# DeltaNet and SwiGLU on one core: splitting float64 weights with a ScalarE multiply and an integer add

## The chip, the cores and the metric

The kernel runs on one core of a Trainium2 chip. The metric is the device time of one execution in microseconds (us). Engines are called as in the profile: PE (TensorE, matrix products; PEld is its weight load), DVE (VectorE), ACT (ScalarE), POOL (GpSimd) and SP (SyncE, which here only issues DMA transfers). A "q" behind a name (SPq, ACTq) is that engine's own instruction queue.

## The reference

Two blocks run one behind the other. The first is a recurrent attention (DeltaNet) over 768 steps for 4 batches and 8 heads of 48; its output is regrouped into 3072 tokens of 384 and goes through a normalised SwiGLU feed-forward of width 1536.

```python
k_n = k / (np.linalg.norm(k, axis=-1, keepdims=True) + 1e-06)
for t in range(S):
    y[:, :, t] = np.einsum('bhd,bhde->bhe', q[:, :, t], state)
    v_old = np.einsum('bhde,bhd->bhe', state, kt)
    state = state + bt[:, :, :, None] * np.einsum('bhd,bhe->bhde', kt, vt - v_old)
...
xn = x / np.sqrt(np.mean(x * x, axis=-1, keepdims=True) + 1e-06) * rms_g
g = xn @ w_gate
out = (g * (1.0 / (1.0 + np.exp(-g))) * (xn @ w_val)) @ w_out
```

The three weight matrices (`w_gate` and `w_val` 384 x 1536, `w_out` 1536 x 384) arrive as float64. The kernel computes in float32, so it has to turn each weight into a float32, and there is no float64 arithmetic on the engines: the two 32-bit words of each number are worked on apart.

## The kernel before, in words

**Chunks.** The 768 steps are cut into 12 chunks of 64 (`NCH`). For each chunk, `prep(c)` solves the small triangular systems inside the chunk, `qpart(c)` makes the masked scores of q, and `recur(c)` applies the chunk to the running state and makes the chunk's rows of x, which are 256 tokens. Each chunk's tokens then go through the feed-forward: `ffn_plain` for chunks 0 and 1 (L1094 up, L1076 down) and `ffn` with `down` for the others (L1187 and L1244), which use sums and differences of weight blocks made by `factors` and `out_factors` and so fewer products.

**The preparation of a chunk** is a chain over many engines. The scores of k (L546) go out to DRAM (buffer dkk) and come back in another layout as `at` (L659). VectorE scales `at` (L665) and solves the system in a scan of 15 steps, two instructions each (L712 and L718), some 16 us in all. ScalarE copies the result apart (L735, only the first two chunks use it in this form), it goes to DRAM (buffer dx) and comes back in small transfers as `mt` (for chunk 1 `mt` lies in the tile `wsum`, so the profile says wsum) and `x2bd`. PE turns a block (L770), VectorE and ScalarE copy it to `m1bd` (L783, L781), two merges follow on PE (L794 and L818) with copies behind them (L804; L832 and L834), and `mt` is whole. Then `recur` multiplies it with the residual (L905), copies to `u` (L942, L944), multiplies by the scores (L919), and brings the rows to unit mean square (L981 or L987 and L993, root on POOL L1006, scaling L1014 or L1021); PE turns them (L1027), ScalarE scales them by the weights of the norm (L1031), and the feed-forward can begin.

**The weights** are loaded in 18 pieces of 768 KB (`weights`, loads 0 to 17) through three raw buffers (`raw`, number n mod 3) and two pairs of conversion buffers (`cva` and `cvb`, n mod 2). In a float64, the upper word has the sign, 11 bits of exponent and 20 of mantissa; the lower word has the other 32 bits of mantissa. Before the change a load is converted in four or five steps:

- ScalarE (L467) reads the upper word as if it were a float32 and scales it by a power of two, another one for negative numbers (a Prelu), which puts the exponent, and the sign with it, where they should be after a shift.
- VectorE (L455) shifts that word left by three. Now it is the float32 of the weight with its mantissa cut at 20 bits: `top`.
- VectorE (L458) masks sign and exponent of `top` into `cc`.
- VectorE (L463) multiplies the lower word (taken as a number) by 2**-52 and by `cc`: the part of the weight that was cut off.
- The two parts are added: for the first three loads by two PE products with the identity into one PSUM bank (L480, L481) and a ScalarE copy out of it (L485), for the other 15 by one VectorE add (L488).

A raw buffer is free for the next load once L463 has read it.

**The order of the work** is not that of the code. Each operation is put on a list with an engine, an estimated duration, a priority, the data it reads and writes and the PSUM banks it takes (`Plan.add`). `Plan.run` plans all engines forward and backward 60 times, with small random shakes of the priorities from a fixed seed, and writes out the order with the earliest planned end; each engine, and SP's queue of transfers, then runs its instructions strictly in that order. So an operation that is added or removed, or whose estimate changes, can move any other. Up to a planned 70 us, the holes that the plan leaves on PE are filled with products of the identity with itself (`filler`, L1344), which keep it busy and compute nothing.

Of the kernel before, what the change touches and what calls it, by code (L numbers as in the profile page):

```python
# [12 lines left out]
U32 = mybir.dt.uint32  # L13
I64 = mybir.dt.int64
ALU = mybir.AluOpType
# [234 lines left out]
def kernel(  # L250
# [17 lines left out]
    nc = tc.nc  # L268
# [14 lines left out]
    def sbt(name, shape, n=None, dt=FP32):  # L283
        if n is None:
            return sb.tile(shape, dt, name=name)
        return [sb.tile(shape, dt, name=f"{name}{i}") for i in range(n)]

    ident = sbt("ident", [128, 128])
# [15 lines left out]
    NPE, NRAW, NCV = 3, 3, 2  # L304
# [39 lines left out]
    tmp = sbt("tmp", [128, 6, 512])  # L344
# [4 lines left out]
    raw = [more[:, 1536 * i : 1536 * i + 1536].bitcast(I64) for i in range(NRAW)]  # L349
    cvb = [tflat[:, 512:1280], more[:, 4608:5376]]  # L350
    cva = [xf[:, 6:12].rearrange("p a n -> p (a n)"), more[:, 5376:6144]]
# [9 lines left out]
    P = Plan()  # L361
    V = lambda n: 0.13 + 0.0011 * n
    VF = lambda n: 0.13 + 0.0006 * n
    A = lambda n: 0.2 + 0.0008 * n
    G = lambda n: 0.15 + 0.0022 * n

    def dma(dst, src, prio, r=(), w=(), work=0.3, dur=0.5, eng="SP", after=0.0):
        queue = nc.scalar if eng == "ACT" else nc.sync
        op = P.add(eng, dur, lambda: queue.dma_start(out=dst, in_=src), prio, r, w, lat=0.7)  # L369
        op.dma, op.work, op.ready = True, work, after  # L370
# [50 lines left out]
    def spot(f):  # L421

        return f // 6 * 6 + (0, 1, 4, 5, 2, 3)[f % 6]


    def weights():
        todo = []
        for half_ in range(2):
            c0 = half_ * WCOL

            for i_ in range(3):
                for side, (key, w) in enumerate((("wg", moe_w_gate), ("wv", moe_w_val))):
                    c1 = c0 + 256 * i_
                    src = w.rearrange("(t p) c -> p t c", p=128)[:, :, c1 : c1 + 256]
                    todo.append((w_in[:, side, half_, i_:9:3], src, [(key, half_, i_)]))
                if i_:
                    for f in ((6 * half_,) if i_ == 1 else (6 * half_ + 2, 6 * half_ + 4)):
                        src = moe_w_out[f * 128 : f * 128 + 256, :].rearrange("(a p) c -> p a c", a=2)
                        z = spot(f)
                        todo.append((wo_sb[:, z : z + 2], src, [("wo", f), ("wo", f + 1)]))  # L440
        for n, (dst, src, keys) in enumerate(todo):
            pr = (30 if n < 9 else CV2) + 0.2 * n
            i, a = n % NRAW, n % NCV
            parts = dst.shape[1]
            rdst = raw[i].rearrange("p (a c) -> p a c", a=parts)
            dma(rdst, src, (0.1 if n == 0 else 3 + 2 * n), w=[("raw", i)], dur=0.7, work=3.06, after=(7.5, 5.0, 19.2, 27.2, 24.5, 33.3, 47.0)[n] if n < 7 else 48.8)

            low, high = (raw[i].bitcast(U32)[:, w_ : w_ + 2 * WCOL - 1 : 2] for w_ in range(2))
            top, cc = cva[a], cvb[a]
            u = top.bitcast(U32)  # L450
            tiled = lambda t: t.rearrange("p (a n) -> p a n", a=parts)
            cak, cvk = [("cva", a)], [("o", 1)] if a else [("tmp", 1), ("tmp", 2)]

            def s2(u=u):
                nc.vector.tensor_scalar(out=u, in0=u, scalar1=3, scalar2=None, op0=ALU.logical_shift_left)  # L455

            def s4(u=u, cc=cc):
                nc.vector.tensor_scalar(  # L458
                    out=cc.bitcast(U32), in0=u, scalar1=0xFF800000, scalar2=None, op0=ALU.bitwise_and
                )  # L460

            def s5(low=low, cc=cc, by=2.0**-52):
                nc.vector.scalar_tensor_tensor(out=cc, in0=low, scalar=by, in1=cc, op0=ALU.mult, op1=ALU.mult)  # L463

            P.add("ACT", 0.84, lambda high=high, top=top: nc.scalar.activation(out=top, in_=high.bitcast(FP32), func=ACTF.Prelu, scale=2.0**-112, alpha=2.0**32), pr, r=[("raw", i)], w=cak)  # L467
            P.add("DVE", 0.57, s2, pr, w=cak)
            P.add("DVE", 0.57, s4, pr, r=cak, w=cvk)
            P.add("DVE", 0.96, s5, pr, r=[("raw", i)], w=cvk)  # L470
            done = []
            if n < NPE:
                for x_ in range(2):
                    ps = Group()
                    cut = slice(2 * x_, 2 + x_)
                    flat = slice(512 * x_, 512 + 256 * x_)
                    m = 512 - 256 * x_

                    def s6(ps=ps, top=top[:, flat], cc=cc[:, flat], m=m):
                        nc.tensor.matmul(ps.t[:, 0:m], ident, top, start=True, stop=False)  # L480
                        nc.tensor.matmul(ps.t[:, 0:m], ident, cc, start=False, stop=True)  # L481

                    P.add("PE", 0.0035 * m, s6, pr, r=cvk + cak + ["ident"], w=[("cvp", n, x_)], ps=ps, size=8)
                    done.append(("cv", n, x_))
                    P.add("ACT", A(m), lambda dst=dst[:, cut], ps=ps, m=m: nc.scalar.copy(dst, ps.t[:, 0:m].rearrange("p (a n) -> p a n", n=256)), pr, r=[("cvp", n, x_)], w=[done[-1]], last=ps)  # L485
            else:
                done.append(("cv", n))
                P.add("DVE", 0.97, lambda dst=dst, top=tiled(top), cc=tiled(cc): nc.vector.tensor_tensor(out=dst, in0=top, in1=cc, op=ALU.add), pr, r=cvk + cak, w=[done[-1]])  # L488
            for key in keys:
                ready.setdefault(key, []).extend(done)  # L490

# [581 lines left out]
    def down_mm(po, f, f0, f1):  # L1073
        def mm():
            for p in range(2):
                nc.tensor.matmul(  # L1076
                    po[p].t[:, 0:DM], hf[:, spot(f), 128 * p : 128 * p + 128], wo_sb[:, spot(f)], start=(f == f0), stop=(f == f1 - 1),
                    skip_group_check=True,
                )

        return mm

    def ffn_plain(c, f0, f1, start):
        x_, xk = (xp1, [("x1", 0), ("x1", 1)]) if c else (xf, [("xp", 0), ("xp", 1)])
        po = [Group(), Group()]

        def up(f):
            ps = Group()
            h_, i_, n = f // 6, f % 6 // 2, 128 * (f % 2)
            for side, key in enumerate(("wg", "wv")):  # L1090

                def mm(side=side, ps=ps):
                    for t in range(KT):
                        nc.tensor.matmul(  # L1094
                            ps.t[:, TOK * side : TOK * side + TOK], w_in[:, side, h_, 3 * t + i_, n : n + 128],
                            x_[:, 2 * t : 2 * t + 2].rearrange("p a n -> p (a n)"), start=(t == 0), stop=(t == KT - 1)
                        )

                P.add("PE", 1.31, mm, start + 3.9 * (f - f0), r=xk + [("wuse", h_)] + ready[(key, h_, i_)], w=[ps, (("sil", f % 2), ("hf", f, 0))[side]], ps=ps, size=12)
            a = f % 2  # L1100
            P.add("ACT", A(256), lambda ps=ps: nc.scalar.activation(out=sil[a], in_=ps.t[:, 0:TOK], func=ACTF.Silu), -1, r=[ps], w=[("sil", a)], last=ps)
            P.add("DVE", V(256), lambda ps=ps: nc.vector.tensor_tensor(out=hf[:, spot(f)], in0=sil[a], in1=ps.t[:, TOK : 2 * TOK], op=ALU.mult), -1, r=[("sil", a), ps, ("tmp", 0)], w=[("hf", f, 0), ("hf", f, 1)], last=ps)

        def down(f):
            if f == f0:
                P.add("PE", 0.0, lambda: None, start, r=xk + [("cvp", n, x_) for n in range(NPE) for x_ in range(2)], w=["po"], ps=po[1])
            P.add("PE", 1.31, down_mm(po, f, f0, f1), start + 3.9 * (f - f0) + 9, r=[("hf", f, 0), ("hf", f, 1), "wouse"] + ready[("wo", f)], w=["po"], ps=po[0], size=8)

        LAG = 2
        for f in range(f0, f1 + LAG):  # L1110
            if f < f1:
                up(f)
            if f >= f0 + LAG:
                down(f - LAG)
        finish(c, po, f0, f1)
# [179 lines left out]
    load(0, "kqv")  # L1295
    load_small()
    weights()
    load(1, "k")
    P.slack, P.lead = 0.0, 1000.0
# [80 lines left out]
```

## Time and profile before

| | |
|---|---|
| median of 3 runs | 716.01 us (714.25 to 716.3) |
| span of the profiled execution, first to last instruction | 713.4 us |
| PE busy | 694.6 us (97%) |
| DVE busy | 553.9 us (78%) |
| ACT busy | 303.5 us (43%) |
| of PE: fillers (L1344) | 43.1 us |
| VectorE conversion: L455, L458, L463, L488, one each, 128 x 768 | 0.56, 0.56, 0.96, 0.95 us |
| ScalarE conversion: L467, 128 x 768 | 0.92 us |

The span is from the profiled execution alone; its device time is not listed apart, so it is compared with the median of the runs. In a row of the profile, the text names the line, the engine, the operation and the tiles (what is written, an arrow, what is read), then come the shape, the count, the busy time and the mean of one in ns, and at the end the idle time of the engine before these instructions with what ended it. In a row of busy times by stretches, the two times are followed by the length, the busy time of PE, PEld, DVE, ACT and POOL with the number of instructions, the granted PE clock as a share of full speed, the busy share of the DMA engines, and what they moved in GB/s.

### The profile page before, as it was taken

What the parts mean: (1) busy time and instruction counts of PE and PEld (TensorE: products, weight loads), DVE (VectorE), ACT (ScalarE), POOL (GpSimd) and SP (SyncE); (2) the same over time, 40 slices, a digit from 0 to 9 for tenths busy, and PEclk for the clock granted to TensorE, in tenths of its full rate; (3) what the DMA queues carried; (4) which work ended last, traced back from release to release, by engine and by line L of the source; (5) the groups of instructions that cost most, each with busy time, mean ns of one, the idle gap of its engine ahead of it and who ended that gap; (6) DMA issues with size and microseconds to landing.
All of it is one profiled execution on the core that took longest, in us unless ns stands there. A gap on an engine that the chain in (4) does not pass through costs nothing.

```text
span 713.4 us, 23227 instructions
## 1 busy us (share of the span) xinstructions
PE 694.6 (97%) x9950; PEld 630.5 (88%) x9950; DVE 553.9 (78%) x1148; ACT 303.5 (43%) x712; POOL 138.2 (19%) x140
## 2 busy tenths in 40 slices
PE   8999698999999999999999999999999999999997
PEld 5657576787879999999999999999999999999997
DVE  4899788999949949949949959959937969947373
ACT  5335353233415634534525535435345444345231
POOL 4202103102131231231232232232105040100000
PEclk9999889999999999999999999999999999999999
DMA  7886898262540170262451361450461170030000
GB/s 142 229 140 134 174 270 185 32 110 38 94 82 13 26 126 17 49 104 38 65 102 32 61 119 25 77 89 11 62 121 22 16 121 7 21 58 2 23 1 23
DMA packets 232791, 54.67 MB, mean 77 GB/s; under 512 B 221936, under 2 KB 225008, under 8 KB 232688
## 3 DMA queue, kind: packets, MB, share of 16 engines
q1 hardware_dynamic: 227840, 52.27, 39.2%
q10 hardware_dynamic: 4848, 0.92, 0.9%
q8 instruction: 78, 1.28, 0.8%
q14 instruction: 25, 0.20, 0.1%
HBM read 40.83 MB, written 12.32 MB: 75 GB/s over the span
## 4 chain that ended last, share of the span: by engine, by line
PE 84%; DVE 6%; DMA 3%; issue 3%; SPq 2%; POOL 1%; ACT 0%; POOLq 0%; DVEq 0%; ACTq 0%
PE bank L1187 35%; PE bank L1244 19%; PE bank L1094 8%; PE bank L1076 4%; PE bank L546 3%; PE bank L1344 3%; PE bank L859 3%; PE bank L905 2%; PE bank L818 2%; SPq L369 2%; PE bank L919 2%; DVE tmp L1197 1%; PE bank L523 1%; DMA dx<-wsum 1%; PE bank L794 1%
## 5 line engine op out<-in xcount | busy, mean ns | idle before, releaser
L1187 PE MATMUL bank<-xf,w_in 128*128 128x128 f32 x1440 | 180.8, 277 | 0.0
L1197 DVE TENSOR_TENSOR tmp<-tmp,bank 128x512 f32<-128x512 f32 x180 | 121.4, 683 | 69.4 <-PE bank L1187 62.8
L1187 PEld LDWEIGHTS bank<-xf,w_in 128*128 128x128 f32 x1440 | 170.0, 192 | 2.4 <-issue 1.2
L1187 PE MATMUL bank<-xf,more 128*128 128x128 f32 x960 | 125.0, 277 | 0.3 <-DVE tmp L1197 0.3
L1187 PEld LDWEIGHTS bank<-xf,more 128*128 128x128 f32 x960 | 115.4, 192 | 2.3 <-DVE tmp L1197 0.5
L1199 ACT COPY tmp<-bank 128x512 f32<-128x512 f32 x120 | 68.9, 586 | 91.3 <-PE bank L1187 65.6
L718 DVE TENSOR_REDUCE acc<-acc 128x30 f32<-128x90 f32 (+4 forms) x180 | 85.1, 473 | 6.2
L1203 ACT ACTIVATE tmp<-tmp 128x256 f32<-128x256 f32 x120 | 49.8, 418 | 88.0 <-DVE tmp L1197 87.5
L568 POOL TENSOR_TENSOR knrm<-ksum,half 128x16 f32<-128x16 f32 x12 | 36.1, 3011 | 195.9 <-DVE ksum L567 195.9
L712 DVE TENSOR_TENSOR acc<-acc,at 128x60 f32<-128x60 f32 (+4 forms) x180 | 63.2, 351 | 6.5 <-DMA out_dram<-tmp 3.8
L1244 PE MATMUL bank<-wo_sb,hf 128*128 128x192 f32 x360 | 63.9, 327 | 0.0
L1204 DVE TENSOR_TENSOR hf<-tmp 128x256 f32<-128x256 f32 x120 | 52.7, 453 | 7.9 <-ACT tmp L1203 7.3
L1244 PEld LDWEIGHTS bank<-wo_sb,hf 128*128 128x128 f32 x360 | 58.2, 190 | 0.3
L1344 PE MATMUL bank<-ident 128*128 128x128 f32 (+2 forms) x150 | 43.1, 433 | 1.4 <-POOL ident masks.py:199 1.4
L1344 PEld LDWEIGHTS bank<-ident 128*128 128x128 f32 x150 | 25.4, 195 | 17.8 <-issue 15.2
L1094 PE MATMUL bank<-xf,w_in 128*128 128x256 f32 x144 | 36.1, 400 | 3.2 <-issue 2.8
L1094 PEld LDWEIGHTS bank<-xf,w_in 128*128 128x128 f32 x144 | 28.1, 200 | 10.0 <-issue 3.9
L739 POOL COPY acc<-acc 128x128 f32<-128x128 f32 x40 | 19.8, 526 | 85.6 <-DVE acc L718 85.2
L665 POOL TENSOR_TENSOR at<-at,beta_b 128x1024 f32<-128x1024 f32 x8 | 18.8, 2355 | 88.0 <-DMA at<-dkk 63.0
L1076 PE MATMUL bank<-wo_sb,hf 128*128 128x384 f32 x96 | 35.6, 508 | 0.0
L1094 PE MATMUL bank<-xp,w_in 128*128 128x256 f32 x144 | 33.3, 382 | 0.0
L1094 PEld LDWEIGHTS bank<-xp,w_in 128*128 128x128 f32 x144 | 26.8, 190 | 4.5
(167 smaller groups left out, 1006.3 us busy)
## 6 DMA issues: line engine op xcount, KB each, us to landing
at<-dkk SPq DMA_DIRECT2D x23, 256.0 KB, 4.4
more<-in_moe_w_val_dram SPq DMA_DIRECT2D x6, 768.0 KB, 6.5
more<-in_moe_w_gate_dram SPq DMA_DIRECT2D x6, 768.0 KB, 7.2
more<-in_moe_w_out_dram SPq DMA_DIRECT2D x6, 768.0 KB, 7.6
vt<-in_v_dram SPq DMA_DIRECT2D x24, 192.0 KB, 4.5
out_dram<-tmp SPq DMA_DIRECT2D x48, 96.0 KB, 2.2
k<-in_k_dram SPq DMA_DIRECT2D x23, 192.0 KB, 4.0
mt<-dx SPq DMA_DIRECT2D x84, 32.0 KB, 2.1
```

The lines of the kernel that those rows point to most:

```text
L568: P.add("POOL", 2.95, lambda: nc.gpsimd.tensor_tensor(out=knrm[i2], in0=ksum[i2], in1=half, op=ALU.pow), pn, r=[("ksum", i2), "half"], w=[ ...
L712: nc.vector.tensor_tensor(out=acc[:, 1:3, 0:n, j + 2 : W].rearrange("p a i t -> p i a t"), in0=acc[:, old, 0:n, j : j + 2, None].to_broadc ...
L718: nc.vector.tensor_reduce(out=acc[:, new, 0:n, j + 2 : W], in_=acc[:, lo : lo + 3, 0:n, j + 2 : W].rearrange("p a i t -> p i t a"), axis=A ...
L1076: nc.tensor.matmul(po[p].t[:, 0:DM], hf[:, spot(f), 128 * p : 128 * p + 128], wo_sb[:, spot(f)], start=(f == f0), stop=(f == f1 - 1), skip ...
L1094: nc.tensor.matmul(ps.t[:, TOK * side : TOK * side + TOK], w_in[:, side, h_, 3 * t + i_, n : n + 128], x_[:, 2 * t : 2 * t + 2].rearrange( ...
L1187: nc.tensor.matmul(g.t[:, 128 * z : 128 * z + 128], fac[:, side, 128 * f : 128 * f + 128], xf[:, xs], start=(begin and z == 0), stop=False ...
L1197: P.add("DVE", V(512), lambda t=t, g=g: nc.vector.tensor_tensor(out=t, in0=t, in1=g.t, op=ALU.add), -1, r=[g], w=[tk], last=g)
L1199: P.add("ACT", A(512), lambda t=t, g=g: nc.scalar.copy(t, g.t), -1, r=[g], w=[tk], last=g)
L1203: P.add("ACT", A(256), lambda t=t: nc.scalar.activation(out=t[:, 0:256], in_=t[:, 0:256], func=ACTF.Silu), -1, w=[tk])
L1204: P.add("DVE", V(256), lambda t=t, f0=f0, p=p: nc.vector.tensor_tensor(out=hf[:, spot(f0) : spot(f0) + 2, 128 * p : 128 * p + 128], in0=t[ ...
L1244: nc.tensor.matmul(g.t[:, 0:192], a_[:, f], b_[:, f], start=(begin and f == 0), stop=(f == 5), skip_group_check=True)
L1344: nc.tensor.matmul(warm[:, 0 : 128 * w_].rearrange("p (w n) -> p w n", n=128), ident, ident[:, None, :].to_broadcast([128, w_, 128]))
```

## The change

The conversion of a load becomes four instructions, and the same four for all 18 loads: ScalarE's Prelu as before; a second ScalarE instruction, which reads the lower word as an unsigned integer, multiplies it by 2**-29 and writes an unsigned integer between 0 and 8 (the lower word in units of the last place of the float32); VectorE's shift of the upper word as before; and a VectorE add of the two as 32-bit integers into the weight tile. The mask, the VectorE multiply, the float add, and the PE products and ScalarE copies of the first three loads go. The raw buffer is now last read by ScalarE. In `ffn_plain`, the first operation no longer names the PE products of the conversion among what it waits for.

```diff
-            def s4(u=u, cc=cc):
-                nc.vector.tensor_scalar(
-                    out=cc.bitcast(U32), in0=u, scalar1=0xFF800000, scalar2=None, op0=ALU.bitwise_and
-                )
-
-            def s5(low=low, cc=cc, by=2.0**-52):
-                nc.vector.scalar_tensor_tensor(out=cc, in0=low, scalar=by, in1=cc, op0=ALU.mult, op1=ALU.mult)
...
             P.add("ACT", 0.84, lambda high=high, top=top: nc.scalar.activation(out=top, in_=high.bitcast(FP32), func=ACTF.Prelu, scale=2.0**-112, alpha=2.0**32), pr, r=[("raw", i)], w=cak)
-            P.add("DVE", 0.57, s2, pr, w=cak)
-            P.add("DVE", 0.57, s4, pr, r=cak, w=cvk)
-            P.add("DVE", 0.96, s5, pr, r=[("raw", i)], w=cvk)
-            done = []
-            if n < NPE:
...
-                    def s6(ps=ps, top=top[:, flat], cc=cc[:, flat], m=m):
-                        nc.tensor.matmul(ps.t[:, 0:m], ident, top, start=True, stop=False)
-                        nc.tensor.matmul(ps.t[:, 0:m], ident, cc, start=False, stop=True)
...
-            else:
-                done.append(("cv", n))
-                P.add("DVE", 0.97, lambda dst=dst, top=tiled(top), cc=tiled(cc): nc.vector.tensor_tensor(out=dst, in0=top, in1=cc, op=ALU.add), pr, r=cvk + cak, w=[done[-1]])
+            P.add("ACT", 0.84, lambda low=low, r=r: nc.scalar.mul(r, low, 2.0**-29), pr, r=[("raw", i)], w=cvk)
+            P.add("DVE", 0.57, lambda u=u: nc.vector.tensor_scalar(out=u, in0=u, scalar1=3, scalar2=None, op0=ALU.logical_shift_left), pr, w=cak)
+            P.add("DVE", 0.93, lambda dst=dst, u=tiled(u), r=tiled(r): nc.vector.tensor_tensor(out=dst.bitcast(U32), in0=u, in1=r, op=ALU.add), pr, r=cvk + cak, w=[("cv", n)])
+            done = [("cv", n)]
...
             if f == f0:
-                P.add("PE", 0.0, lambda: None, start, r=xk + [("cvp", n, x_) for n in range(NPE) for x_ in range(2)], w=["po"], ps=po[1])
+                P.add("PE", 0.0, lambda: None, start, r=xk, w=["po"], ps=po[1])
```

The new file is 30 lines shorter; below the conversion, a line of the kernel before has a number that is 30 higher than the same line after. The conversion's lines after the change are L454 (Prelu), L455 (ScalarE multiply), L456 (shift) and L457 (integer add).

More of the change, by code (lines that the diff above doesn't have):

```diff
@@ L449, in weights @@
             top, cc = cva[a], cvb[a]
-            u = top.bitcast(U32)
+            cak, cvk = [("cva", a)], [("o", 1)] if a else [("tmp", 1), ("tmp", 2)]
+            u, r = top.bitcast(U32), cc.bitcast(U32)
             tiled = lambda t: t.rearrange("p (a n) -> p a n", a=parts)
-            cak, cvk = [("cva", a)], [("o", 1)] if a else [("tmp", 1), ("tmp", 2)]
-            def s2(u=u):
-                nc.vector.tensor_scalar(out=u, in0=u, scalar1=3, scalar2=None, op0=ALU.logical_shift_left)
@@ L468, in weights @@
-            P.add("DVE", 0.57, s2, pr, w=cak)
-            P.add("DVE", 0.57, s4, pr, r=cak, w=cvk)
-            P.add("DVE", 0.96, s5, pr, r=[("raw", i)], w=cvk)
-            done = []
-            if n < NPE:
[L473 to L477, printed above, removed]
-                    def s6(ps=ps, top=top[:, flat], cc=cc[:, flat], m=m):
-                        nc.tensor.matmul(ps.t[:, 0:m], ident, top, start=True, stop=False)
-                        nc.tensor.matmul(ps.t[:, 0:m], ident, cc, start=False, stop=True)
-                    P.add("PE", 0.0035 * m, s6, pr, r=cvk + cak + ["ident"], w=[("cvp", n, x_)], ps=ps, size=8)
-                    done.append(("cv", n, x_))
-                    P.add("ACT", A(m), lambda dst=dst[:, cut], ps=ps, m=m: nc.scalar.copy(dst, ps.t[:, 0:m].rearrange("p (a n) -> p a n", n=256)), pr, r=[("cvp", n, x_)], w=[done[-1]], last=ps)
-            else:
-                done.append(("cv", n))
-                P.add("DVE", 0.97, lambda dst=dst, top=tiled(top), cc=tiled(cc): nc.vector.tensor_tensor(out=dst, in0=top, in1=cc, op=ALU.add), pr, r=cvk + cak, w=[done[-1]])
```

## The prediction

> **What bounds the kernel now.** I read the page first, then busy time by stretches, the waits of TensorE, and the timeline from 20 to 120 us.
>
> ```profile
> span 713.4 us, 23227 instructions
> PE 694.6 (97%) x9950; PEld 630.5 (88%) x9950; DVE 553.9 (78%) x1148; ACT 303.5 (43%) x712; POOL 138.2 (19%) x140
> ```
>
> TensorE (PE) is the bound. Yet up to 70 us much of its work is filler (L1344, 43.1 us on the page). So what counts is when its real work starts to run without holes. Busy time by stretches (start:end, length, PE, PEld, DVE, ACT, POOL, granted clock, DMA share, GB/s), then the waits of TensorE from 60 us on:
>
> ```profile
> 0.00:70.00 70.00, 65.94 (x846) 44.19 (x847) 56.24 (x123) 32.66 (x71) 14.49 (x19) 1.00 0.76 164
> ...
> 80.00:90.00 10.00, 3.56 (x118) 3.12 (x121) 5.86 (x12) 4.05 (x8) 0.00 (x0) 0.67 0.91 200
> ...
> 100.00:120.00 20.00, 17.24 (x302) 12.68 (x301) 18.44 (x33) 9.71 (x23) 5.53 (x3) 0.91 0.89 188
> ...
> 160.00:211.00 51.00, 51.00 (x688) 40.17 (x688) 38.87 (x80) 17.07 (x42) 12.40 (x13) 1.00 0.45 74
> ```
>
> The waits (how long, how often, the longest):
>
> ```profile
> PE bank L770 <- DMA wsum<-dx: 6.4, 1, 6.4
> PE bank L1094 <- issue: 2.8, 1, 2.8
> PE bank L1094 <- ACT xf L1031: 0.5, 1, 0.5
> ```
>
> From 120 us to the tail TensorE has no hole over 1 us. The holes lie between 70 and 111 us; the largest is the wait of L770 for the small transfers (DRAM buffer dx to mt, which lies in wsum for chunk 1) that end the preparation of chunk 1. Its chain in the timeline (start, length):
>
> ```profile
> 49.44 1.22 DVE L665 TENSOR_TENSOR at<-at,beta_b 128x1024 f32<-128x1024 f32 x1
> ...
> 55.62 0.84 DVE L783 COPY m1bd<-bank 32x256 f32<-32x256 f32 x2
> ...
> 67.62 0.78 ACT L735 COPY wsum<-acc 128x256 f32<-128x256 f32 x2
> ...
> 71.34 6.91 PE L1094 MATMUL bank<-xf,w_in 128*128 128x256 f32 x30 [0.46 <-ACT xf L1031]
> ...
> 75.92 1.93 SPq L369 DMA_DIRECT2D dx<-wsum  x2
> ...
> 80.47 1.99 SPq L369 DMA_DIRECT2D wsum<-dx  x4
> ```
>
> Chunk 1's scan starts at 49.44 (L665), because VectorE converted loads 2, 3 and 4 from 40.90 to 49.5. It is spread by ScalarE at 67.62, but SP issues dx only at 75.92: sixteen loads of q, two of v and two of k stand before it. L770 starts at 86.87. Meanwhile chunk 0's chain, whose m1bd copies VectorE makes in the middle of chunk 1's scan, has opened the first feed-forward matmul at 71.34.
>
> **The change part by part.** Durations, grouped by shape up to 160 us:
>
> ```profile
> L463 DVE SCALAR_TENSOR_TENSOR tmp<-more,tmp 128x768 f32<-128x768 uint32 x9 | 8.6, 956 | 0.2
> ...
> L458 DVE TENSOR_SCALAR tmp<-xf 128x768 uint32<-128x768 uint32 x9 | 5.0, 557 | 0.3
> ...
> L488 DVE TENSOR_TENSOR w_in<-xf,tmp 128x768 f32<-128x768 f32 x4 | 3.8, 938 | 0.0
> ...
> L665 DVE TENSOR_TENSOR at<-at,beta_b 128x1024 f32<-128x1024 f32 x3 | 3.7, 1220 | 0.0
> ...
> L467 ACT ACTIVATE more<-more 128x768 f32<-128x768 f32 x9 | 8.3, 923 | 9.6 <-DMA more<-in_moe_w_val_dram 6.2 <-DVE w_in L488 2.0 <-DMA more<-in_moe_w_gate_dram 1.3
> ```
>
> Removed: 18 masks (0.56) and 18 multiplies (0.96), 27.4 us of VectorE; 12 matmuls with the identity of the first three loads, which stand among fillers before 50 us and so cost nothing (the filler takes their place); six ScalarE copies (3 of 0.59, 3 of 0.37, 2.9 us).
>
> Added: 18 ScalarE multiplies. No row has one with uint32 in and out. From below 0.84 (L564, dense 128x768), from above 0.92 (L467, which also reads every second word). I take 0.92, the same reading: 16.6 us. ScalarE is 43% busy, so this is paid only where it queues ahead of a chain, below.
>
> Three more adds, and all 18 adds are now an integer add. The built program's listing shows it as an instruction of a kind of its own over 1536 elements where the words number 768. No row shows it. From below 0.56 (L458, one source, 768 words). From above 1.75: 128x512 takes 0.695 (L695) and 128x1024 1.22, so 1.03 ns an element, 512 more elements than 1024. I take 0.95, L488, the same bytes from the same buffers. The Trainium skill, VectorE: DVE Perf Modes, the perf-mode tier table, gives two-source operations two elements a cycle in 16-bit data and one in fp32; its formula would make that (768+151)/0.96 = 957 ns, an estimate, and 1757 ns at one a cycle. No run here shows which holds.
>
> VectorE saves 27.4 - 3 x 0.95 = 24.6 us in all, but what counts is order. The raw buffer is freed by ScalarE instead of VectorE, so loads need not wait for a scan to end; the planner, seeing this, rearranges every queue. In the built program:
>
> - VectorE converts four loads (2 to 5) between the scans, not three, then runs chunk 1's scan unbroken, and only then chunk 0's m1bd copies.
> - SP has issued 11 weight loads before chunk 1's dx instead of 8 (one of them before v, at the place of about 33 us; it was 44.25); the v loads and one k go behind dx.
> - Before chunk 1's L1027, TensorE has in both programs the same work: 36 groups of two L1094, 10 of two L1076, equal transposes and scores. So all that is left after it is equal, and a shift there goes through to the end.
>
> Start of the scans. Load 0: shift 0.56 after the norms, add 0.95 at 22.9, L665 at 23.9 instead of 24.38 (-0.5). Scan of chunk 0 as before 16.2 (24.38 to 40.57): to 40.1. Then ScalarE: spread 0.93, L670 1.05, L676 0.66, issue of dx 0.59, to 43.3; the two ops each of loads 4 and 5, 4 x 0.91, to 46.9; the last add to 47.9. VectorE itself would need only 4 x 1.51 = 6.0, to 46.1. at was issued up to 44.16, last landing 43.2 + 5.1 = 48.3 at worst. Scan of chunk 1 from 48.0 (before 49.44), 16.2 unbroken, to 64.2 (before 67.62): -3.4.
>
> Chunk 0's chain. Its m1bd copies move from 55.62 to 64.2. From there to the first L1094 it was 15.7, of which 2.2 was TensorE's filler (yn was ready at 67.75, L1027 at 69.96): 13.5 without. ScalarE now has six conversion ops of loads 8 to 10 (5.5 us) among the chain's own; I put three on the path (9's second, both of 10, which stand between the squares and the scaled copies), 2.7, and 0.3 for VectorE's conversions ahead of L834: first L1094 at 80.7 instead of 71.34. Nothing is lost by that alone, since the 30 L1094 instructions (6.9) lie before the L770 wait: they end at 87.6.
>
> Chunk 1's transfers. From the first weight load behind mt (53.08) to dx it was 22.8. v and one pair of k go (-3.7), two more weight issues and one k come (+0.8): 19.9, starting 1.1 later as ScalarE's half of dx is behind L670 and L676: dx at 74.1. To L770 another 10.95, plus 1.1 for v, k and a load between dx and mt on SP, plus about 1.0 for their bytes: 87.2. So both gates come at 87.2 to 87.6; L770 at 87.6, +0.7.
>
> Clock: the granted clock is 0.50 from 84 to 92 us, after the hole, and the 6.6 us of work from 86.87 to 93.5 lose half: 3.3. Now the thin stretch is before the 30 matmuls, and I charge the same 3.3 there: L770 at 90.9. The Trainium skill, TensorE: Matmul & The Clock Gate, Part 1, says an idle window of about 3.4 us halves the clock and as much busy time restores it; the trace agrees in kind, with about 7 us to restore. By that rule, if each hole stays under 3.4 us, nothing is charged, and the sum falls by 3.3.
>
> From L770 to the end of chunk 1's L919 it was 20.8 (86.87 to 107.7) with that 3.3 in it, so 17.5; the new order has three more L1094 groups and one L546 less there, 18.4. That ends at 109.3: +1.6. VectorE's work between L944 and L987 (5.75) shortens by 0.55. Sum +1.1: span 714.5. The median of the runs, 716.01, lies 2.6 over the profiled span of 713.4 (the execution's own time is not listed, so the 2.6 holds start and end too); with it 717.1.
>
> **The rivals.**
> 1. The earlier scan goes through. For it: VectorE loses 24.6 us, and the DMA share from 60 to 72 us is only 0.18 to 0.49, room for the moved loads. Against it: dx waits in SP's queue, not for VectorE. If dx lands so that L770 is ready at 84.0 and the first L1094 comes by 77, with no hole long enough for the clock, L919 ends at 84.0 + 18.4 = 102.4, -5.3: 710.7.
> 2. The integer add takes 1.75. For it: 1536 elements. Against: the bytes of L488. Four adds before the scan (+3.2), then those of loads 6 to 9 on chunk 0's chain (+3.2): 6.4 less 0.4 of waiting for at, +6.0: 723.1.
> 3. SP's queue becomes the bound: three more loads of 768 KB before dx, and an issue waits for the transfer eight before it (eight transfer semaphores in the listing). 768 KB take 2.2 to 3.1 us at the 346 and 246 GB/s of the busy stretches, so up to 9.3; about half fits in the free DMA share. +4.5: 721.6. It decides from dx later than 77.
> 4. Nothing reaches TensorE: the gate stays, as with a change that does not touch the path: 716.0.
>
> **How the numbers follow.** Forecast 0.40, rivals 0.25, 0.12, 0.15 and 0.08. The forecast's own range is 713.5 to 721 (2 us either way on each gate, and a dense part whose order is new as well). 0.3% is 2.15 us, about what a measurement here can tell. Faster: 0.05 of the forecast and 0.23 of rival 1, 0.28. Within: 0.20, 0.02 of rival 1 and 0.07 of rival 4, 0.29. Slower: 0.15, rivals 2 and 3, 0.01 of rival 4, 0.43. The range takes in rival 1 and most of 2: 709.5 to 724.
>
> **What would show it.** The integer add at 0.95 or 1.75; ScalarE's multiply at 0.92; chunk 1's spread near 64; first L1094 near 80; dx near 74; L770 near 90 with little wait before it; L919 of chunk 1 ending near 109; the granted clock between 75 and 95. New holes of TensorE after 120 us, where I count none, would make it wrong, and so would a dx that follows its spread at once.

## The result, and the profile after

The changed kernel takes 719.91 us (median of 20 runs, 715.64 to 725.14), the kernel before in the runs taken with them 715.26 us (20 runs, 712.09 to 717.63). The ratio is 1.0066 with an interval of 1.0047 to 1.0086: slower by two thirds of a per cent. Below the conversion, a line of the changed kernel has the old number less 30 (L770 is now L740, L1094 is L1064, L1027 is L997, L1187 is L1157, L1197 is L1167).

The page of the changed kernel, its first two lines on busy time:

```profile
span 716.6 us, 23156 instructions
...
PE 700.2 (98%) x9940; PEld 631.0 (88%) x9940; DVE 533.4 (74%) x1115; ACT 314.0 (44%) x724; POOL 137.5 (19%) x140
```

VectorE has 20.5 us less to do, and the span is 3.2 us longer. (This execution took 718.33 us, 1.7 over its span. It is the sixth quickest of the 20, so the two profiles show 3.2 of the 4.65 us between the medians.) The new instructions, from the groups by shape up to 160 us:

```profile
L455 ACT ACTIVATE tmp<-more 128x768 uint32<-128x768 uint32 x9 | 8.3, 918 | 0.0
...
L457 DVE CUSTOM_DVE_ANT_0 w_in<-more 128x1536 uint16<-128x1536 uint16 x6 | 5.7, 956 | 2.3 <-ACT more L455 2.0
...
L457 DVE CUSTOM_DVE_ANT_0 wo_sb<-more 128x1536 uint16<-128x1536 uint16 x3 | 2.9, 954 | 0.4 <-ACT more L455 0.2
```

The integer add takes 0.95 to 0.96 us (one of the 18 took 1.26), so its 1536 halves of words pass at the pace of 768 words. The Trainium skill (VectorE: DVE Perf Modes, the perf-mode tier table) gives two-source operations twice the rate in bf16 that they have in fp32; the prediction's estimate from it was 957 ns, and the trace agrees with that time. The stretches that the prediction showed of before:

```profile
0.00:70.00 70.00, 66.53 (x573) 39.59 (x574) 52.89 (x114) 35.04 (x58) 12.18 (x16) 0.98 0.79 186
80.00:90.00 10.00, 8.41 (x99) 7.37 (x98) 3.23 (x6) 8.24 (x18) 0.00 (x0) 0.96 0.79 148
100.00:120.00 20.00, 18.39 (x311) 13.11 (x310) 15.16 (x31) 14.06 (x30) 5.21 (x4) 1.00 0.88 203
160.00:211.00 51.00, 51.00 (x599) 40.66 (x598) 29.50 (x68) 15.17 (x38) 12.87 (x13) 1.00 0.35 61
```

From 80 to 90 us TensorE works 8.41 us at a clock of 0.96, where it was 3.56 at 0.67: the gap that was the largest of the kernel before is closed. Its waits from 60 us on:

```profile
PE bank L926 <- issue: 2.9, 2, 2.5
PE bank L1157 <- DVE tmp L1167: 2.0, 1, 2.0
PE bank L997 <- ACT yn L991: 1.6, 1, 1.6
PE bank L764 <- DVE m1bd L753: 1.6, 1, 1.6
PE bank L516 <- issue: 1.6, 1, 1.6
PE bank L1214 <- DVE pt L559: 0.5, 1, 0.5
PE bank L1214 <- DVE tmp L1223: 0.3, 1, 0.3
```

The 6.4 us of L770 are gone. In their place stand several of 1.6 to 2.5 (the 2.9 of L926 are two waits), and one of them, L1157's 2.0, lies late. The chain in the timeline, up to chunk 1's turn of x:

```profile
48.29 1.22 DVE L635 TENSOR_TENSOR at<-at,beta_b 128x1024 f32<-128x1024 f32 x1
...
64.79 0.84 DVE L753 COPY m1bd<-bank 32x256 f32<-32x256 f32 x2
...
71.50 2.03 SPq L369 DMA_DIRECT2D dx<-wsum  x2
...
82.26 4.67 SPq L369 DMA_DIRECT2D wsum<-dx  x4
...
84.19 6.74 PE L1064 MATMUL bank<-xf,w_in 128*128 128x256 f32 x30
...
90.86 1.11 PE L740 MATMUL bank<-ident,wsum 32*32 32x32 f32 x64
...
115.97 1.05 PE L997 MATMUL bank<-ident,yn 128*128 128x128 f32 x6 [1.60 <-ACT yn L991]
```

L740 follows the 30 feed-forward products without a wait. Then comes the turn: chunk 1's L997 runs at 115.97 us, where L1027 ran at 117.59 before:

```profile
117.59 0.82 PE L1027 MATMUL bank<-ident,yn 128*128 128x128 f32 x6
```

**The changed kernel is 1.6 us ahead there, and ends 3.2 us later.** What is left takes 600.6 us instead of 595.8. The one large hole in it, in the timeline of TensorE and then of VectorE:

```profile
477.26 1.16 PE L1157 MATMUL bank<-xf,w_in 128*128 128x128 f32 x8
480.42 2.07 PE L1157 MATMUL bank<-xf,more 128*128 128x128 f32 x8 [2.00 <-DVE tmp L1167]
```

```profile
475.86 0.22 DVE L682 TENSOR_TENSOR acc<-acc,at 128x60 f32<-128x60 f32 x1 [3.42 <-DMA out_dram<-tmp]
...
479.23 0.54 DVE L688 TENSOR_REDUCE acc<-acc 128x110 f32<-128x330 f32 x1
479.69 0.68 DVE L1167 TENSOR_TENSOR tmp<-tmp,bank 128x512 f32<-128x512 f32 x1
```

VectorE stood idle for 3.42 us, because ten instructions of a scan (L682 and L688) stand ahead of the add L1167 in its order, and the scan's input came from GpSimd (L665, which is L695 in the kernel before) only at 475.82. (The profile names a transfer as what ended the wait; that one had nothing to do with `acc`.) The add was held behind them, and with it the PSUM banks that L1157 needs. The granted clock was then 0.50 from 480.2 to 483.6 us, which costs another 1.7 by estimate, half of these 3.4. Holes of over 0.25 us after 120 us add up to 3.24 us in the changed kernel and to 0.72 before, so holes and clock make 4.2 of the 4.8 us.

### The profile page after: what moved, and what is told of

Its sections match the earlier page's. It is cut to its first block, busy times and chain, and to the rows that moved or that the text cites. A ratio compares the mean times of both kernels' runs of the same rounds, so it can differ in the third digit from the quotient of the medians.

```text
span 716.6 us, 23156 instructions
## 1 busy us (share of the span) xinstructions
PE 700.2 (98%) x9940; PEld 631.0 (88%) x9940; DVE 533.4 (74%) x1115; ACT 314.0 (44%) x724; POOL 137.5 (19%) x140
## 4 chain that ended last, share of the span: by engine, by line
PE 77%; DVE 10%; DMA 5%; SPq 4%; issue 2%; ACT 1%; POOL 1%; DVEq 0%; POOLq 0%; ACTq 0%
PE bank L1157 35%; PE bank L1214 17%; PE bank L1064 7%; SPq L369 4%; PE bank L1046 3%; DVE acc L688 3%; PE bank L516 3%; PE bank L829 3%; DMA more<-in_moe_w_out_dram 2%; DVE acc L682 2%; PE bank L875 2%; PE bank L788 2%; PE bank L889 2%; DVE tmp L1167 1%; PE bank L493 1%
## 5 line engine op out<-in xcount | busy, mean ns | idle before, releaser
L1157 PE MATMUL bank<-xf,w_in 128*128 128x128 f32 x1440 | 181.1, 277 | 0.0
L1157 PEld LDWEIGHTS bank<-xf,w_in 128*128 128x128 f32 x1440 | 170.1, 192 | 2.0 <-issue 0.6
L1167 DVE TENSOR_TENSOR tmp<-tmp,bank 128x512 f32<-128x512 f32 x180 | 120.7, 682 | 66.1 <-PE bank L1157 58.0
L1157 PE MATMUL bank<-xf,more 128*128 128x128 f32 x960 | 126.2, 279 | 2.0 <-DVE tmp L1167 2.0
L1157 PEld LDWEIGHTS bank<-xf,more 128*128 128x128 f32 x960 | 116.0, 193 | 4.7 <-DVE tmp L1167 2.4
L688 DVE TENSOR_REDUCE acc<-acc 128x30 f32<-128x90 f32 (+4 forms) x180 | 85.0, 472 | 6.2
L682 DVE TENSOR_TENSOR acc<-acc,at 128x60 f32<-128x60 f32 (+4 forms) x180 | 62.8, 349 | 8.8 <-DMA out_dram<-tmp 3.4
L1314 PE MATMUL bank<-ident 128*128 128x512 f32 (+2 forms) x164 | 56.6, 498 | 1.4 <-POOL ident masks.py:199 1.4
L1174 DVE TENSOR_TENSOR hf<-tmp 128x256 f32<-128x256 f32 x120 | 50.5, 437 | 7.7 <-ACT tmp L1173 7.2
L1314 PEld LDWEIGHTS bank<-ident 128*128 128x128 f32 x164 | 29.7, 200 | 27.0 <-issue 24.7
L1223 DVE TENSOR_TENSOR tmp<-tmp,bank 128x192 f32<-128x192 f32 x30 | 10.5, 351 | 33.2 <-PE bank L1214 33.2
L1064 PE MATMUL bank<-xf,w_in 128*128 128x256 f32 x144 | 33.6, 385 | 0.0
L1064 PE MATMUL bank<-xp,w_in 128*128 128x256 f32 x144 | 33.5, 384 | 0.0
L1046 PE MATMUL bank<-wo_sb,hf 128*128 128x384 f32 x96 | 33.0, 488 | 0.0
L1064 PEld LDWEIGHTS bank<-xf,w_in 128*128 128x128 f32 x144 | 26.7, 190 | 4.5 <-issue 0.4
```

The costliest lines, as they stand in the source:

```text
L682: nc.vector.tensor_tensor(out=acc[:, 1:3, 0:n, j + 2 : W].rearrange("p a i t -> p i a t"), in0=acc[:, old, 0:n, j : j + 2, None].to_broadc ...
L688: nc.vector.tensor_reduce(out=acc[:, new, 0:n, j + 2 : W], in_=acc[:, lo : lo + 3, 0:n, j + 2 : W].rearrange("p a i t -> p i t a"), axis=A ...
L1046: nc.tensor.matmul(po[p].t[:, 0:DM], hf[:, spot(f), 128 * p : 128 * p + 128], wo_sb[:, spot(f)], start=(f == f0), stop=(f == f1 - 1), skip ...
L1064: nc.tensor.matmul(ps.t[:, TOK * side : TOK * side + TOK], w_in[:, side, h_, 3 * t + i_, n : n + 128], x_[:, 2 * t : 2 * t + 2].rearrange( ...
L1157: nc.tensor.matmul(g.t[:, 128 * z : 128 * z + 128], fac[:, side, 128 * f : 128 * f + 128], xf[:, xs], start=(begin and z == 0), stop=False ...
L1167: P.add("DVE", V(512), lambda t=t, g=g: nc.vector.tensor_tensor(out=t, in0=t, in1=g.t, op=ALU.add), -1, r=[g], w=[tk], last=g)
```

## The experiments

Two theories at first. A: the instructions cost nothing; the plan, made anew with them, is a worse order of everything, late work included. B: the new instructions themselves cost it, by ScalarE's second pass and by the add.

**The new conversion in the old order.** The old operations stay on the plan's list with their old estimates, but issue the new instructions or nothing; every other instruction of every engine stands where it stood.

```diff
+            def words(high=high, top=top, low=low, r=r):
+                nc.scalar.activation(out=top, in_=high.bitcast(FP32), func=ACTF.Prelu, scale=2.0**-112, alpha=2.0**32)
+                nc.scalar.mul(r, low, 2.0**-29)
...
+            P.add("DVE", 0.57, none, pr, r=cak, w=cvk)
+            P.add("DVE", 0.96, add_ if n < NPE else none, pr, r=[("raw", i)], w=cvk)
```

> The new conversion's instructions in the old order: the plan is made with the estimates and dependencies of the kernel before, and each instruction of every engine and of SP's queue stands where it stood, except that the second ScalarE instruction is written behind the Prelu, the integer add stands in the place of the multiply (loads 0 to 2) or of the float add, and the mask, the products with the identity and the copies behind them are left out. Theory A (the order): the instructions cost nothing on the path, and the loss of the change lies in the new order, whose holes after 116 us (3.3 us, and 1.7 us of halved clock) the kernel before does not have. Then this kernel is at the time before or up to 3 us under it: 712 to 716, no hole over 1 us after 120 us. Theory B (the price): the 16.6 us that ScalarE has more, or the conversion's own chain, cost the time; then it is slower by 3 us or more, 718 to 721, with the delay before 120 us.

Measured: 713.55 us, ratio 0.9977 (0.996 to 0.9994). The change of arithmetic by itself makes the kernel a little faster; B falls. This version is also the only one whose interval lies below 1. In its profile chunk 1's turn of x comes at 114.64 us, 3.0 ahead of the kernel before, and what is left takes 596.7 us. It has one hole over 1 us after 120 us, of 1.07 at 606.7, where none was expected.

**Other draws of the plan.** `Plan.run` shakes its priorities from a fixed seed (47). Three other seeds, for both kernels:

```diff
-        rng = random.Random(47)
+        rng = random.Random(48)
```

> The changed kernel with another seed of the planner's shakes (48 for 47), all else equal, so another order of the same work. Theory A (the order): the loss belongs to the one order that the plan ended in, so another seed gives another time, anywhere in 710 to 725, and the holes after 116 us lie in other places or are gone. Theory B (the price): the time stays at 718 to 722, as the instructions are the same.

> The kernel before with seed 48 for 47. Theory A (the order): the kernel before owes its dense stretch to its order too; another seed moves it by several us, likely up, 715 to 722. Theory B (the price): it stays within 2 us of the kernel before, 713 to 717.

> The changed kernel with seed 49 for 47. Theory A (the order): a third time for the same instructions, 710 to 725, differing from seeds 47 and 48 by 2 us or more. Theory B (the price): 718 to 722 as with 47.

> The kernel before with seed 49. If the seeds of the kernel before all give dense late stretches (seeds 47 and 48: 0.7 and 1.5 us of holes after 116 us) then 712 to 716; if its seeds spread as those of the changed kernel do (ratios 1.0066, 1.0019, 1.0070), 714 to 720.

> The changed kernel with seed 50. If plans made with the new conversion are worse in general: 716 to 722. If it is the luck of one plan: anywhere in 711 to 722, with a time that goes with the holes after 116 us and the halved clock behind them.

> The kernel before with seed 50; as for seed 49: 712 to 716 if the old conversion's plans are dense in general, 714 to 720 if it is the luck of one plan.

| seed | old conversion | new conversion |
|---|---|---|
| 47 | 1 | 1.0066 (1.0047 to 1.0086) |
| 48 | 0.9994 (0.9976 to 1.0012) | 1.0019 (0.9995 to 1.0044) |
| 49 | 1.0006 (0.9986 to 1.0026) | 1.007 (1.0045 to 1.0095) |
| 50 | 1.0007 (0.9993 to 1.002) | 1.0075 (1.0051 to 1.0099) |

Old orders lie within 0.1% of each other. Of four orders planned with the new conversion three are slower by 0.7%, and the fourth can't be told from no change. So it is not the bad luck of one draw; A has to be narrowed to "plans made with the new conversion tend to be worse". Taken alone the seeds fit B better than A as it was stated: the old conversion did not move, and with the new one only seed 48 did, while 49 came within 1 us of 47. It is the first experiment that excludes B. The profiles of the seeds, one each, go with the narrowed A: holes of TensorE over 0.25 us after 120 us add up to 0.3 us with the new conversion and seed 48, and to 5.5 and 3.9 with seeds 49 and 50; with the old conversion they are 1.5, 2.5 and 2.2.

**One add moved.** In the changed kernel, the add L1167 of the hole at 478 us goes ahead of the five scan steps; nothing else on VectorE moves.

```diff
+        late = [x for x in seq if 2060 <= x[0].n <= 2064]
+        seq = [x for x in seq if not 2060 <= x[0].n <= 2064]
+        k_ = [x[0].n for x in seq].index(1923) + 1
+        seq[k_:k_] = late
```

> The changed kernel with one VectorE instruction moved: the feed-forward add that TensorE waited 2.0 us for at 478 us (L1167) is put in front of the first five scan steps (ten instructions) of that chunk, which wait for a late transfer; nothing else changes place on any engine. Theory A (the order): that hole and the 3.4 us of halved clock behind it (1.7 us) were the change's largest single late loss; without it the ratio to the kernel before falls from 1.0066 by 0.002 to 0.005, to 1.002 to 1.005, and the profile shows no hole near 478. Theory C (the hole is only where a lateness shows that comes from elsewhere): TensorE waits as long a little later, and the ratio stays at 1.005 to 1.008.

Measured: 718.82 us, 1.0039 (1.0024 to 1.0055). The interval overlaps that of the changed kernel, so the gain is not settled by the times alone. Nor is it by the profiled span, 716.5 us after 716.6: this execution has 3.4 us of halved clock from 117.3 us on, which the other lacks. In the trace the hole at 478 us and the halved clock behind it are gone, and part of the gain is given back a few microseconds later, by three smaller waits, two of them for tiles of the same sums:

```profile
482.74 0.21 PE L521 MATMUL bank<-qt,kt 64*64 64x64 f32 x1 [0.55 <-issue]
...
489.24 2.05 PE L1162 MATMUL bank<-xf,w_in 128*128 128x128 f32 x16 [0.73 <-ACT tmp L1174]
...
492.81 1.38 PE L1162 MATMUL bank<-xf,more 128*128 128x128 f32 x10 [0.44 <-DVE tmp L1172]
```

**Which part of the order.** The two orders are cut and joined: as far as one TensorE instruction in the order of one kernel, behind it all that remains in the order of the other. In place of planning, the kernel holds the list.

```diff
-        self.first_priorities()
...
+        by = {op.n: op for op in self.ops}
+        best = 0.0, [(by[n], s) for n, s in zip(ORDER, START)]
```

The first pair has its seam at chunk 1's turn of x, about 116 us.

> The changed kernel's instructions in the changed kernel's order up to chunk 1's first L997 (about 116 us), and from there in the order of the kernel before. Theory L (the loss sits in the late order: what is left after chunk 1 is the same work but stands in a worse order): ratio 0.996 to 1.000, the stretch after chunk 1's L997 back at about 596 us against 600.6 in the changed kernel. Theory E (the early order costs it, by the state in which it leaves buffers, transfers and the clock): ratio 1.004 to 1.009. Theory M (neither order is worse by itself, but a late order fits only the early part that it was made with): both mixed kernels are slower than their unmixed ones, this one above 1.002.

> The counterpart: the new conversion's instructions in the old order up to chunk 1's first L1027 (as in the kernel of the first experiment, which ran at 0.9977), and from there every engine in the changed kernel's order. Theory L: 1.003 to 1.008, with holes of TensorE after 120 us as in the changed kernel (3.25 us of holes and 1.7 us of halved clock there, 1.5 us and none in the first experiment). Theory E: 0.996 to 1.000. Theory M: above 1.002 here and in the other mixed kernel.

Measured: new then old 716.78 us, 1.0025 (1.0002 to 1.0047), and no hole over 0.5 us after 120. That is more than theory L expected (0.996 to 1.000) and less than theory E did; in the profile, what is left after chunk 1's turn of x takes 597.9 us, against 600.6 in the changed kernel. Old then new: 732.16 us, 1.0233 (1.0206 to 1.0261). The second says nothing of the late order, because the seam itself made a wait: two conversions lay on different sides of it, and one product of chunk 1's feed-forward stood 12.48 us for its input.

```profile
114.33 0.82 PE L1007 MATMUL bank<-ident,yn 128*128 128x128 f32 x6
127.64 2.93 PE L1056 MATMUL bank<-wo_sb,hf 128*128 128x384 f32 x4 [12.48 <-DVE hf L1082]
```

The second pair has its seam at 258 us of the plan, where all conversions are over in both orders.

> The changed kernel's instructions in the changed kernel's order as far as one TensorE instruction of chunk 3's feed-forward (its L1157, planned at 258 us), and behind it in the order of the kernel before; all conversions lie ahead of this seam in both orders, and only five instructions stand on different sides of it. Theory L (the loss sits in the late order, where the changed kernel's trace has its holes at 335, 412, 478 and 566 us): 0.996 to 1.001, no hole over 1 us and no halved clock after 260 us. Theory E (the early order costs it): 1.005 to 1.008. Theory S (both have a share, as the first mixed kernel's 1.0025 says): 1.002 to 1.005, between the two, without the late holes.

> The counterpart with the same seam: the new conversion in the old order as far as that instruction (as in the kernel of the first experiment, at 0.9977), behind it every engine in the changed kernel's order. Theory L: 1.004 to 1.008, with the holes of TensorE after 260 us and the halved clock of the changed kernel. Theory E: 0.996 to 1.000. Theory S: 0.999 to 1.004; its excess over 0.9977 and that of the other mixed kernel then add up to about the changed kernel's 0.9 per cent over the first experiment.

(In both kernels that go from the old to the new order, one VectorE add of 0.95 us, which makes `xp` for the last products, stands last of all, behind those products, so the last output is computed from another `xp`. From the last chunk's turn of x to the end it is 57.4 us in the kernel with the seam at 258, and 57.0 in the changed kernel.)

Measured: new then old 715.18 us, 0.9996 (0.9975 to 1.0018); old then new 721.65 us, 1.0087 (1.006 to 1.0114). With the late part exchanged, the changed kernel loses its 0.66%, and the fast kernel of the first experiment goes from 0.9977 to 1.0087, a little over what theory L expected. Busy time by stretches, first new then old, then old then new:

```profile
260.00:470.00 210.00, 210.00 (x3303) 204.11 (x3303) 164.32 (x361) 99.84 (x239) 55.74 (x55) 1.00 0.39 65
470.00:500.00 30.00, 30.00 (x515) 29.12 (x514) 25.57 (x54) 14.05 (x32) 5.06 (x4) 1.00 0.17 28
```

```profile
260.00:470.00 210.00, 208.24 (x3306) 201.44 (x3305) 168.52 (x358) 96.43 (x234) 51.92 (x52) 1.00 0.40 66
470.00:500.00 30.00, 27.76 (x507) 26.67 (x505) 22.97 (x49) 10.90 (x23) 10.38 (x7) 0.94 0.09 23
```

In the old late order TensorE has no hole from 260 to 500 us. In the new one it is idle for 1.76 and 2.24 us there, at a clock of 0.94 in the second stretch. The timeline of old then new has the same ten scan instructions ahead of the same add (L1177 there) as the changed kernel:

```profile
478.66 0.22 DVE L692 TENSOR_TENSOR acc<-acc,at 128x60 f32<-128x60 f32 x1 [3.43 <-POOL at L675]
...
482.50 0.68 DVE L1177 TENSOR_TENSOR tmp<-tmp,bank 128x512 f32<-128x512 f32 x1
...
483.23 2.06 PE L1167 MATMUL bank<-xf,more 128*128 128x128 f32 x8 [2.24 <-DVE tmp L1177]
```

Here the profile does name GpSimd's `at` as what the scan waits for. So theory L holds, and the place of the loss with seed 47 is shown: the order planned for the chunks from 3 on, far behind the last conversion.

Between the profiled spans of old then new and of the first experiment, 720.3 and 711.4 us, lie 8.9 us. TensorE's order is the same in both up to 264 us, and 1.5 us have arisen by then, so these are not of the late order. From there to its last product TensorE takes 449.9 us instead of 442.9. Of these 7.0 us the holes of over 0.25 us (4.56 against 1.07) and the halved clock (1.7 by estimate) explain 5.2; where the other 1.9 lie was not found. The remaining 0.4 lie behind the last product. The other pair, the changed kernel and new then old, has one order up to 266 us and takes 446.7 and 442.2 us from there to the last product.

Two things stay open. The early order may have a small share: both kernels that join the new early to the old late order, 1.0025 and 0.9996, lie above the 0.9977 of the old order throughout, but the last two intervals overlap; and old then new, with the better early order, is at 1.0087 no faster than the changed kernel. And what in the plan's input makes its late orders worse was not tried: the raw buffer that comes free earlier, the lower load of VectorE, or the transfers that move with them.

## Why the prediction was right or wrong

The time, 717.1 forecast and 719.91 measured, lies in the range. The prices came out, and so did the two places at 90.9 and 109 us, the first by errors that cancel. That the kernel is slower, as forecast, is luck: at chunk 1's turn of x it was ahead, and the loss came from something that the prediction had ruled out.

- **Prices.** Integer add forecast 0.95, measured 0.95 to 0.96; ScalarE multiply 0.92, measured 0.905 to 0.918. Rival 2 falls.
- **Chunk 0's scan** was to start 0.5 us earlier, at 23.9. It started at 25.14, after 1.17 us of waiting for `at`: VectorE was free earlier, the transfer was not. **Chunk 1's** starts at 48.29 (48.0 forecast), and ends with chunk 0's m1bd copies at 64.79 (64.2).
- **The transfers.** dx was issued at 71.50, not 74.1, but its way back (wsum from dx) began only at 82.26. The step "19.9 from the first weight load to dx" took 17.5 (54.02 to 71.50). What follows was too short: from dx the sum allowed 13.1 us, to 87.2, and the last of the first four transfers of the way back landed at 89.07, 17.6 behind dx. Rival 3, which was to decide from dx later than 77, does not apply by its own sign, though a part of it is seen: two weight loads, v and a k stood in SP's queue between dx and its way back.
- **The first L1064** was to come at 80.7 and came at 84.19. From chunk 0's m1bd copies it took 19.4 us, not 16.5. The sum left out 2.45 and 1.59 us in which TensorE had work ahead of it and waited for nothing that the profile names ("issue", at 74 and 81.6 us).
- **The clock.** 3.3 us were charged on top of the 30 products, which were to run from 80.7 to 87.6; they ran at the full clock (1.00 from 82 to 92). It was halved from 67.2 to 70.6 and from 77.5 to 80.9, ahead of them. TensorE was busy throughout the second of these stretches, so about 1.7 us of clock, an estimate (half of 3.4), are already in the 3.5 by which L1064 came late. The 3.5 stand in the place of the 3.3: 84.19 + 6.74 gives L740 at 90.9 as forecast, by two errors that cancel.
- **L889 of chunk 1** ended at 109.0 (109.3 forecast; 107.8 before). From there to chunk 1's turn of x it took 7.0 us instead of 9.8, where the sum allowed a gain of 0.55: the "issue" hole of 2.76 us at 108.2 and the halved clock behind it (110.8 to 114.2), both of the kernel before, are gone.
- **The step that failed** is "all that is left after it is equal, and a shift there goes through to the end". The work left is equal, its order is not. The prediction compared what stands ahead of chunk 1's L1027 and did not look at how the late order moved, although it says that the planner rearranges every queue. Chunk 1's L997 came 1.6 us earlier than before (the +1.2 at L889's end had turned round by then), and the rest took 4.8 us longer. The exchange of the late orders shows this in both directions.
- Its own test, "New holes of TensorE after 120 us, where I count none, would make it wrong", was met: 3.24 us of them.
- **Rival 1** saw rightly that the new arithmetic can help: in the old order it gains 0.23%, though no run shows that VectorE's lower load is the reason. It sought the gain in the earlier scan, and the earlier scan with the new plan brought 1.6 us by 116 us, not 5.3 by 102.
- **Rival 4**, that nothing reaches TensorE, falls: the gate of L770 went, and chunk 1's turn of x moved by 1.6 us.
- **The median over the span**, put at 2.6 us, is 1.7 in the profiled execution.

## What to carry to other kernels

When a program plans its own order, a cheaper instruction is two changes: the instruction, and a new order of everything. Measure them apart by issuing the new instructions in the old order; here this was worth 0.9% against letting the planner start again, and most of the loss that was found lay hundreds of microseconds behind the last changed instruction. Compare the orders to the end of the program, above all where an engine serves a long chain that waits for transfers (the scan) and short work that frees buffers for the bounding engine (the adds) in one strict queue.

## What the runs showed of the hardware

- A hole of 2.0 us of TensorE can be enough for a halved clock: 0.50 from 480.2 to 483.6 in the changed kernel, from 483.3 to 486.7 in old then new after a hole of 2.24. It need not be: with the new conversion and seed 49 a hole of 2.77 us up to 326.08 us had none behind it, nor had one of 2.40 us up to 78.22 in old then new. Apart from the one that runs into the end, every episode of the halved clock in these two profiles lasts 3.4 us, but for one of 6.8. The Trainium skill (TensorE: Matmul & The Clock Gate, Part 1) gives free-running windows of about 3.4 us, which fits the lengths. By the way in which the prediction used it, that holes under 3.4 us cost nothing, the first two would have been free; they were not.
- A 32-bit integer add on VectorE over 128x768 words costs about the same as a float add of that shape, 0.95 against 0.94 us, though the profile counts it as 1536 elements.
- Over the 20 runs of the changed kernel the time falls with the mean granted clock: 715.64 us at 0.997, 722.63 to 725.14 at 0.988. The clock does not settle it alone: at 0.993 the times go from 718.25 to 723.03. The spread, 9.5 us, is wider than the 5.5 us of the kernel before.
- The "issue" holes of TensorE go with transfers of its instructions. The trace has 78 transfers of 16 KB on the queue that the profile calls "instruction" (q8). Those that started at 73.65 and 80.24 us ended 1.3 and 1.5 us before TensorE went on, and so it is for all 22 "issue" holes over 0.4 us after 30 us in the 14 profiles: each ends 1.2 to 1.7 us behind such a transfer. That it waits for its own instructions there is likely; no run tried it.
